# Taking GpSimd's library operations out of a decode attention kernel: masks from an identity on VectorE, maxima through VectorE transposes, totals through TensorE

## The chip, the cores and the metric

The kernel runs on one core of one Trainium2 chip. The metric is the device time of the slowest core, here the only one, in microseconds (us); lower is better. A core has five engines that run side by side: TensorE (PE in the profile; its weight loads are PEld), VectorE (DVE), ScalarE (ACT), GpSimd (POOL) and SyncE (SP). In this kernel SP issues the loads; 16 DMA engines carry them.

## The reference, cut to what matters

Four sequences each decode one token. The output is `g * a + (1 - g) * b`, where `a` is attention over a long cache and `b` a small gated MLP.

```python
def _A_ref(x, k_cache, v_cache, wq, wo):      # B=4, H=32 heads, Sk=8192 keys, Dh=128, bf16
    q = (x @ wq).reshape(B, Sq, H, Dh).transpose(0, 2, 1, 3)
    scores = jnp.einsum("bhqd,bhkd->bhqk", q, k_cache) * (Dh ** -0.5)
    p = _softmax(scores, axis=-1)
    o = jnp.einsum("bhqk,bhkd->bhqd", p, v_cache)
    return o.transpose(0, 2, 1, 3).reshape(B, Sq, H * Dh) @ wo
...
    g = _sigmoid((x * gate_w).sum(-1, keepdims=True))
    return g * a + (1 - g) * b
```

What matters is the size of the caches: K and V are 268 MB each, every byte is used once, and there is one query per head.

## The kernel before: the parts that the argument touches

Four heads of K (or of V) are one *pair* of loads. A pair fills two of the five slots of a ring in SBUF, 4.19 MB a slot. If the two slots are neighbours, the pair is a single load of 8.39 MB (line 194 of the kernel before); otherwise it is two loads of one slot each (line 198).

```python
NS = 5                                        # slots of the ring
def load_pair(src, n, apart=False):
    a = slots(2)
    if a + 1 < NS and not apart:
        lo = a * RING
        nc.sync.dma_start(out=flat[:, lo:lo + 2 * n], in_=src)              # L194: the whole pair
        return [flat[:, lo:lo + n], flat[:, lo + n:lo + 2 * n]]
    halves = [ring[:, a], ring[:, (a + 1) % NS]]
    for i, half in enumerate(halves):
        nc.sync.dma_start(out=half[:, 0:n], in_=src[:, i * n:(i + 1) * n])  # L198: one slot
    return halves
```

A K pair is worked off in eight chunks: VectorE transposes a chunk from the ring into one of three buffers, and PE multiplies it with `Z`, the spread-out queries. Four chunks empty one slot. After four K pairs (a *group*, eight groups in all) there is a softmax.

```python
def k_pair(d):                                # RD = 8 chunks, JT = 4 chunks a slot
    ...
    if d + 1 < ND:
        spread(d + 1)                         # L425, GpSimd: the Z of the next pair
    ks = load_pair(kv_view(A_k_cache, d), RING)
    for n in range(RD):
        kn, c = ks[n // JT], n % JT
        flat_t = turned(P, CJ * P)            # one of three buffers TB
        nc.vector.transpose(out=flat_t.bitcast(U32), in_=kn[...].bitcast(U32))       # L443
        for he in range(4):
            for z in range(2):
                nc.tensor.matmul(sps[:, z, :], lhsT=Z[...], rhs=T[...], ...)         # L449
        if n == JT + 2:
            flush_late()                      # runs the deferred reciprocal, among others
    if t == GD - 1:
        softmax(g)

def softmax(g):
    nc.vector.tensor_reduce(out=m1[:], in_=sps, axis=AX.X, op=ALU.max)               # L462
    nc.vector.scalar_tensor_tensor(out=mex[:], in0=mask, scalar=m1[:, 0:1], in1=pen[:], ...)
    nc.gpsimd.partition_all_reduce(gmx[:], mex[:], channels=P, reduce_op=bass_isa.ReduceOp.max)
    nc.vector.tensor_tensor(out=gmm[:], in0=gmx[:], in1=nmask[:], op=ALU.mult)
    nc.vector.tensor_reduce(out=negm[:], in_=gmm[:], axis=AX.X, op=ALU.add)
    nc.scalar.activation(out=PTs[:], in_=sps, func=ACT.Exp, bias=negm[:, 0:1], scale=scale,
                         accum_out=rs[:, 0:1])                                       # L474
    ...
    nc.gpsimd.partition_all_reduce(tot[:], rex[:], channels=P, reduce_op=bass_isa.ReduceOp.add)
    def inverse():
        nc.vector.reciprocal(out=rinv[:], in_=tot[:])                                # L484
    late.append(inverse)
```

A V pair needs only PE (64 matmuls, line 523). At the end of a group's V pairs ScalarE and VectorE scale the sums into `OS` (lines 535 and 536). The masks are made at the start with GpSimd's `affine_select`. TensorE, VectorE and GpSimd run in program order; ScalarE's order is chosen by the scheduler.

Of the kernel before, what the change touches and what calls it, by code (L numbers as in the profile page):

```python
# [9 lines left out]

BF = mybir.dt.bfloat16
F32 = mybir.dt.float32
U32 = mybir.dt.uint32
ACT = mybir.ActivationFunctionType
ALU = mybir.AluOpType
AX = mybir.AxisListType
# [98 lines left out]
def kernel(  # L115
# [15 lines left out]
    nc = tc.nc  # L131
    P = 128
# [4 lines left out]
    NQ = 4  # L137
    QP = P // NQ
    JR = Sk // QP // 2
    CJ = 32  # L140
    JT = JR // CJ
    RD = 2 * JT
    GD = QP // RD
    GH = GD * NQ
    ND = Bn * H // NQ
# [9 lines left out]
    scale = float(Dh) ** -0.5  # L155
# [3 lines left out]
    const = ctx.enter_context(tc.tile_pool(name="const", bufs=1))  # L159
    ptp = ctx.enter_context(tc.tile_pool(name="ptp", bufs=1))  # L160
    stat = ctx.enter_context(tc.tile_pool(name="stat", bufs=2))
# [15 lines left out]
    def turned(rows, n, dtype=BF):  # L177
        t = TB[tb_turn[0] % 3]
        tb_turn[0] += 1
        return t[0:rows, 0:n] if dtype == BF else t[0:rows, 0:2 * n].bitcast(dtype)  # L180
# [8 lines left out]
# [5 lines that stand above are left out]
            nc.sync.dma_start(out=flat[:, lo:lo + 2 * n], in_=src)  # L194
# [3 lines that stand above are left out]
            nc.sync.dma_start(out=half[:, 0:n], in_=src[:, i * n:(i + 1) * n])  # L198
        return halves

    def small(shape, dtype=F32):
        return mps.tile(shape, dtype, name="small", tag="small")
# [14 lines left out]
    for z in (q_ps, o_ps, acc4):  # L217
        nc.vector.memset(z[:], 0.0)
    acc = acc4[0:Bn].rearrange("p z n -> p (z n)")
    ident = const.tile([P, P], F32)  # L220
    make_identity(nc, ident[:])
    identb = const.tile([P, P], BF)
    nc.vector.tensor_copy(out=identb[:], in_=ident[:])
    xw_ps = small([P, DT, NX], BF)
# [3 lines left out]
    nc.vector.tensor_copy(out=xw[:], in_=xw_ps[:])  # L228
    xT = [xw[:, t, 0:Bn] for t in range(DT)]
    R = ptp.tile([P, 4, P], BF, name="R", tag="PTs")  # L230
    nc.gpsimd.memset(R[:], 0.0)
    for he in range(4):
        half, e = divmod(he, 2)
        nc.gpsimd.affine_select(out=R[:, he, :], in_=R[:, he, :], compare_op=ALU.not_equal, fill=1.0,
                                base=-(64 * half + e), pattern=[[0, 4], [-2, 32]], channel_multiplier=1)

    def band(t, width, steps):

        nc.gpsimd.memset(t[:], 1.0)
        nc.gpsimd.affine_select(out=t[:], in_=t[:], compare_op=ALU.is_ge, fill=0.0, base=0,  # L240
                                pattern=[[-s, n] for s, n in steps], channel_multiplier=1)
        nc.gpsimd.affine_select(out=t[:], in_=t[:], compare_op=ALU.is_ge, fill=0.0, base=width - 1,
                                pattern=[[s, n] for s, n in steps], channel_multiplier=-1)

    mask3 = const.tile([P, GD, NQ], F32)
    band(mask3, RD, [(RD, GD), (QP, NQ)])
    mask = mask3[:].rearrange("p t q -> p (t q)")
    pen = const.tile([P, GH], F32)
    nc.vector.tensor_scalar(out=pen[:], in0=mask, scalar1=-1.0, scalar2=3.0e38, op0=ALU.add, op1=ALU.mult)
    nmask = const.tile([P, GH], F32)  # L250
    nc.vector.tensor_scalar(out=nmask[:], in0=mask, scalar1=-scale, scalar2=None, op0=ALU.mult)
    selg = const.tile([P, 4, GD, NQ], F32)
    nc.gpsimd.memset(selg[:], 0.0)
    for e in range(2):
        nc.gpsimd.affine_select(out=selg[:], in_=selg[:], compare_op=ALU.not_equal, fill=1.0,
                                base=-16 * e, pattern=[[-1, 4], [-32, GD], [-4, NQ]], channel_multiplier=1)
    mE4 = const.tile([P, 2, 4], F32)
    band(mE4, 16, [(16, 2), (32, 4)])
    mE = const.tile([P, 2], F32)
    nc.vector.tensor_reduce(out=mE[:], in_=mE4[:], axis=AX.X, op=ALU.add)  # L260
    mq = const.tile([P, 1, NQ], BF)
    band(mq, QP, [(0, 1), (QP, NQ)])
    ZW = QP - 1 + P + 1
    Zt = [const.tile([P, 4, ZW], BF, name=f"Z{i}") for i in range(2)]
    PB = const.tile([P, QP, 2, 2, 2, NQ, 4], BF, name="PB")
# [149 lines left out]
    def heads(d):  # L415
        return divmod(d * NQ, H)

    def kv_view(cache, d):
        b, h0 = heads(d)
        return cache[b, h0:h0 + NQ].rearrange("h (r j) d -> (h r) (j d)", j=2 * JR)  # L420

    def spread(d):
        b, h0 = heads(d)
        Z = Zt[d % 2]
        nc.gpsimd.tensor_tensor(out=Z[:, :, QP - 1:QP - 1 + P].rearrange("p e (q c) -> p e q c", c=QP)[:, :, :, 0],  # L425
                                in0=qa[:, :, h0:h0 + NQ, b], in1=mq[:].to_broadcast([P, 4, NQ]), op=ALU.mult)

    def k_pair(d):
        g, t = divmod(d, GD)
        Z = Zt[d % 2]  # L430
        if d == 0:
            spread(0)
        if d + 1 < ND:
            spread(d + 1)
        if t == 0:
            S_ps[g] = scp.tile([P, 2, 512], F32, name="S_ps")
        sps = S_ps[g]
# [3 lines that stand above are left out]
            flat_t = turned(P, CJ * P)  # L441
            T = flat_t.rearrange("p (j h i e) -> p j h i e", j=CJ, h=2, e=2)
            nc.vector.transpose(out=flat_t.bitcast(U32),  # L443
                                in_=kn[:, c * CJ * Dh:(c + 1) * CJ * Dh].bitcast(U32))
            s = QP - 1 - (RD * t + n)
            for he in range(4):
                half, e = divmod(he, 2)
                for z in range(2):
                    nc.tensor.matmul(sps[:, z, :], lhsT=Z[:, he, s:s + P], rhs=T[:, 16 * z:16 * z + 16, half, :, e],  # L449
                                     start=(t == 0 and n == 0 and he == 0),  # L450
                                     stop=(t == GD - 1 and n == RD - 1 and he == 3))
            if n == JT:
                flush()
            if n == JT + 2:
                flush_late()
        if t == GD - 1:
            softmax(g)

    def softmax(g):
        sps = S_ps.pop(g)  # L460
        m1 = stat.tile([P, 1], F32, tag="m1")
        nc.vector.tensor_reduce(out=m1[:], in_=sps[:].rearrange("p z n -> p (z n)"), axis=AX.X, op=ALU.max)  # L462
        mex = stat.tile([P, GH], F32, tag="mex")
        nc.vector.scalar_tensor_tensor(out=mex[:], in0=mask, scalar=m1[:, 0:1], in1=pen[:],  # L464
                                       op0=ALU.mult, op1=ALU.add)
        gmx = stat.tile([P, GH], F32, tag="gmx")
        nc.gpsimd.partition_all_reduce(gmx[:], mex[:], channels=P, reduce_op=bass_isa.ReduceOp.max)  # L467
        gmm = stat.tile([P, GH], F32, tag="gmm")
        nc.vector.tensor_tensor(out=gmm[:], in0=gmx[:], in1=nmask[:], op=ALU.mult)
        negm = stat.tile([P, 1], F32, tag="negm")  # L470
        nc.vector.tensor_reduce(out=negm[:], in_=gmm[:], axis=AX.X, op=ALU.add)  # L471
        PTs = ptp.tile([P, 1024], BF, name="PTs", tag="PTs")
        rs = stat.tile([P, 1], F32, tag="rs")
        nc.scalar.activation(out=PTs[:], in_=sps[:].rearrange("p z n -> p (z n)"), func=ACT.Exp, bias=negm[:, 0:1], scale=scale, accum_out=rs[:, 0:1])  # L474
        PT = ptp.tile([P, 32, 32], BF, name="PT")
        nc.vector.transpose(out=PT[:].rearrange("p j i -> p (j i)"), in_=PTs[:])  # L476
        rex = stat.tile([P, GH], F32, tag="rex")
        nc.vector.tensor_scalar(out=rex[:], in0=mask, scalar1=rs[:, 0:1], scalar2=None, op0=ALU.mult)
        tot = stat.tile([P, GH], F32, tag="tot")
        nc.gpsimd.partition_all_reduce(tot[:], rex[:], channels=P, reduce_op=bass_isa.ReduceOp.add)  # L480

        def inverse():
            rinv = stat.tile([P, GH], F32, name="rinv", tag="rinv")
            nc.vector.reciprocal(out=rinv[:], in_=tot[:])  # L484
            rinv_t[g] = rinv
        late.append(inverse)

        def spread_p():
            Pv = PT[:].rearrange("p (q j) i -> p i q j", j=4)
            Bv = PB[:].rearrange("p i z w e s j -> p i (z w e) s j")  # L490
            for q in range(NQ):
                at = slice(QP * q, QP * (q + 1))
                if q % 2 == 0:
                    nc.scalar.copy(out=Bv[at, :, :, q, :], in_=Pv[at])  # L494
                else:
                    nc.gpsimd.tensor_copy(out=Bv[at, :, :, q, :], in_=Pv[at])  # L496
        behind.append(spread_p)
# [125 lines left out]
```

## Time and profile before

| what | before |
|---|---|
| time, median of the first 3 runs | 1344.0 us |
| bytes moved, mean rate | 576.18 MB, 429 GB/s |
| PE, DVE, ACT, POOL busy | 77%, 46%, 4%, 4% |

The page of the kernel before: busy time of each engine with its number of instructions, the busy tenths of the 16 DMA engines in 40 equal slices of the run, what they moved, and the shares of the chain of work that ended last.

```profile
span 1342.2 us, 7623 instructions
PE 1031.1 (77%) x4536; PEld 225.1 (17%) x2348; DVE 612.2 (46%) x358; ACT 50.6 (4%) x46; POOL 55.1 (4%) x90
DMA  9999999999999999999999999999999999999998
DMA packets 14316, 576.18 MB, mean 429 GB/s; under 512 B 1598, under 2 KB 1606, under 8 KB 2252
...
DMA 69%; DVE 19%; PE 10%; another core or an unknown queue 1%; issue 0%; ACT 0%; DVEq 0%; SPq 0%
```

The DMA row is the first thing to see: 9 tenths or more in 39 slices of 40. No other engine is near that. The chain still gives VectorE 19%. The next lines, from the chain of the kernel before in order of time (start, length, what), show why: four transposes free a slot, and a K load is issued at once.

```profile
327.45 8.90 DVE TB L443 x4
336.35 0.02 issue
336.37 29.65 DMA ring<-in_A_k_cache_dram
```

Four transposes free a slot at 336.35, a K load is issued at once, and it lands 29.65 us later. The timeline gives this issue as one instruction of line 194, so it is a whole pair of 8.39 MB. At 433 GB/s (the windows from 100 to 1200 us show 432 to 433), that is 19.4 us of transfer. The other 10 us passed mostly behind loads that were already queued: the load issued before it, at 315.02, landed 31.6 us later, at 346.6, and so had 10.3 us to go.

The softmax of one group, in the timeline of the kernel before (start, length, engine, line, operation; in brackets the idle time before it and its releaser):

```profile
618.43 1.22 DVE L462 TENSOR_REDUCE m<-S_ps 128x1 f32<-128x1024 f32 x1 [1.98 <-PE S_ps L449]
619.69 0.23 DVE L464 SCALAR_TENSOR_TENSOR mex<-mask,m,pen 128x16 f32<-128x16 f32 x1
620.06 0.39 POOL L467 PARTITION_ALL_REDUCE gmx<-mex  x1 [40.05 <-DVE mex L464]
620.49 0.18 DVE L469 TENSOR_TENSOR gmm<-gmx,nmask 128x16 f32<-128x16 f32 x1 [0.56 <-POOL gmx L467]
620.70 0.17 DVE L471 TENSOR_REDUCE negm<-gmm 128x1 f32<-128x16 f32 x1
620.90 1.11 ACT L474 ACTIVATE PTs<-S_ps,negm 128x1024 bf16<-128x1024 f32 x1 [136.73 <-DVE negm L471]
...
623.60 0.45 POOL L480 PARTITION_ALL_REDUCE tot<-rex  x1 [3.15 <-DVE rex L478]
624.08 0.25 DVE L484 RECIPROCAL rinv<-tot 128x16 f32<-128x16 f32 x1 [0.58 <-POOL tot L480]
```

The reductions themselves are short. What looks dear on GpSimd is something else: in the waits it sat idle with no releaser for 11.9 us before the first mask operation, and for 75.7 us in 7 cases before a spread that follows a reduction (engine, line, for what: total us, times, longest us):

```profile
POOL Z L425 <- issue: 75.7, 7, 12.3
```

The trace shows instructions named MODIFY_POOL_CONFIG at the reductions (16 records) and at the spreads (14). The Trainium skill ("GPSIMD Engine Reference", 2.1 Instruction dispatch) says that GpSimd's code can be loaded at run time, and that the first call of a freshly loaded one pays about 6 us with no visible instruction. The trace agrees in kind, and shows 10.8 us on average (75.7 / 7).

### The profile page before, as it was taken

How to read it: one execution, taken by the hardware profiler on the slowest of the kernel's cores; microseconds unless marked ns; L12 is line 12 of the kernel's file. 1: busy time of each engine (PE TensorE's matmuls, PEld its weight loads, DVE VectorE, ACT ScalarE, POOL GpSimd, SP SyncE). 2: the span in 40 equal slices, each digit the busy share in tenths (PEclk: the TensorE clock that was granted, in tenths of full speed). 3: DMA queues.
4: the chain of work that ended last, by engine and by line, in shares of the span. 5: the costliest groups of instructions: out<-in, count | busy, mean ns of one | idle time of the engine just before them, and what ended most of it. 6: DMA issues, size and time to landing. Idle time of an engine off the chain costs nothing.

```text
span 1342.2 us, 7623 instructions
## 1 busy us (share of the span) xinstructions
PE 1031.1 (77%) x4536; PEld 225.1 (17%) x2348; DVE 612.2 (46%) x358; ACT 50.6 (4%) x46; POOL 55.1 (4%) x90
## 2 busy tenths in 40 slices
PE   2565877787788687778977779697778679877898
PEld 0111111111111121111211112111111112111221
DVE  1555655544345554335455546146555254556000
ACT  0000100001000010001000010000100010000100
POOL 2000010001000010001000010000100010000100
PEclk9787988988998888899988889898889799889999
DMA  9999999999999999999999999999999999999998
GB/s 414 438 430 428 434 436 427 445 436 416 441 430 427 441 434 426 438 434 430 432 434 426 434 434 432 434 435 438 426 422 438 428 432 438 434 420 447 421 423 337
DMA packets 14316, 576.18 MB, mean 429 GB/s; under 512 B 1598, under 2 KB 1606, under 8 KB 2252
## 3 DMA queue, kind: packets, MB, share of 16 engines
q1 hardware_dynamic: 14276, 575.69, 99.5%
q8 instruction: 27, 0.44, 0.1%
q14 instruction: 5, 0.04, 0.0%
q10 hardware_dynamic: 8, 0.00, 0.0%
HBM read 575.68 MB, written 0.01 MB: 429 GB/s over the span
## 4 chain that ended last, share of the span: by engine, by line
DMA 69%; DVE 19%; PE 10%; another core or an unknown queue 1%; issue 0%; ACT 0%; DVEq 0%; SPq 0%
DMA ring<-in_A_k_cache_dram 56%; DVE TB L443 19%; DMA ring<-in_A_v_cache_dram 10%; PE o_ps L523 7%; PE S_ps L449 2%; DMA x<-in_A_x_dram 2%; DMA ring<-in_A_wo_dram 1%; PE S_ps L313 0%; PE acc L313 0%; PE acc L279 0%; PE small L543 0%; DVE OS L536 0%; ACT OS L535 0%; PE small L226 0%
## 5 line engine op out<-in xcount | busy, mean ns | idle before, releaser
L443 DVE STREAM_TRANSPOSE TB<-ring 128x2048 uint32<-128x2048 uint32 x256 | 567.0, 2277 | 494.6 <-DMA ring<-in_A_k_cache_dram 493.3
L449 PE MATMUL S_ps<-TB,Z 128*128 128x512 bf16 x2048 | 520.0, 410 | 218.5 <-DVE TB L443 218.2
L523 PE MATMUL o_ps<-ring,PB 128*32 128x512 bf16 x2048 | 460.0, 387 | 55.1 <-DMA ring<-in_A_v_cache_dram 50.5
L449 PEld LDWEIGHTS <-Z 128*128 128x128 bf16 x1024 | 105.6, 103 | 628.6 <-issue 627.0
L523 PEld LDWEIGHTS <-PB 128*32 128x32 bf16 x1024 | 100.6, 98 | 411.0 <-issue 402.1
L536 DVE SCALAR_TENSOR_TENSOR OS<-o_ps,mE,OS 128x512 f32<-128x512 f32 x8 | 6.0, 750 | 102.8 <-ACT OS L535 102.8
L474 ACT ACTIVATE PTs<-S_ps,negm 128x1024 bf16<-128x1024 f32 x8 | 8.9, 1113 | 1024.5 <-DVE negm L471 1024.5
L425 POOL TENSOR_TENSOR Z<-qa,mq 128x16 bf16<-128x16 bf16 x32 | 9.0, 285 | 745.1 <-PE S_ps L449 658.0
L496 POOL COPY PB<-PT 32x1024 bf16<-32x1024 bf16 x16 | 30.3, 1896 | 81.1 <-PE o_ps L523 80.7
L494 ACT COPY PB<-PT 32x1024 bf16<-32x1024 bf16 x16 | 30.6, 1909 | 1.5 <-DVE PT L476 1.3
L376 DVE CAST LT<-small 128x64 bf16<-128x64 f32 x2 | 0.4, 224 | 43.0 <-PE small L374 43.0
L226 PE MATMUL small<-identb,x 6*128 6x6 bf16 x8 | 0.7, 201 | 23.0 <-DMA x<-in_A_x_dram 23.0
L467 POOL PARTITION_ALL_REDUCE gmx<-mex x8 | 3.2, 394 | 340.3 <-DVE mex L464 340.3
L462 DVE TENSOR_REDUCE m<-S_ps 128x1 f32<-128x1024 f32 x8 | 9.8, 1224 | 15.9 <-PE S_ps L449 15.9
L279 PE MATMUL acc<-ring,LT 128*4 128x512 bf16 x64 | 14.8, 378 | 1.7 <-DMA ring<-in_A_wo_dram 0.9
L476 DVE STREAM_TRANSPOSE PT<-PTs 128x1024 bf16<-128x1024 bf16 x8 | 10.0, 1245 | 10.2 <-ACT PTs L474 10.2
L279 PE MATMUL acc<-ring,hT 128*4 128x512 bf16 x56 | 12.2, 379 | 0.0
L535 ACT ACTIVATE OS<-o_ps,mE 128x512 f32<-128x512 f32 x8 | 5.5, 687 | 159.0 <-PE o_ps L523 159.0
L313 PE MATMUL o_ps<-ring,xw 128*4 128x512 bf16 x56 | 6.3, 577 | 4.7 <-DMA ring<-in_B_w_gate_dram 4.7
L543 PEld LDWEIGHTS small<-selg,OS 128*128 128x128 f32 x64 | 8.2, 191 | 4.0 <-issue 3.9
L543 PE MATMUL small<-selg,OS 128*128 128x16 f32 x64 | 7.9, 255 | 0.0
L548 DVE SCALAR_TENSOR_TENSOR OT<-small,sgb,rinv 128x16 bf16<-128x16 f32 x8 | 1.8, 222 | 9.6 <-PE small L543 9.6
(71 smaller groups left out, 67.3 us busy)
## 6 DMA issues: line engine op xcount, KB each, us to landing
ring<-in_A_k_cache_dram SPq DMA_DIRECT2D x14, 4096.0 KB, 34.1
ring<-in_A_v_cache_dram SPq DMA_DIRECT2D x14, 4096.0 KB, 31.4
ring<-in_B_w_gate_dram SPq DMA_DIRECT2D x1, 7168.0 KB, 38.0
ring<-in_B_w_up_dram SPq DMA_DIRECT2D x1, 7168.0 KB, 39.2
ring<-in_B_w_down_dram SPq DMA_DIRECT2D x2, 3584.0 KB, 28.0
ring<-in_A_wo_dram SPq DMA_DIRECT2D x6, 1024.0 KB, 24.7
ring<-in_A_v_cache_dram SPq DMA_DIRECT2D x2, 2048.0 KB, 30.9
ring<-in_A_v_cache_dram SPq DMA_DIRECT2D x4, 1024.0 KB, 24.6
```

The source lines that it names most:

```text
L279: nc.tensor.matmul(out_ap, lhsT=lhsT, rhs=rhs, start=start, stop=True, skip_group_check=True)
L313: nc.tensor.matmul(ps[32 * k:32 * k + Bn, z, :], lhsT=xT[TW * half + t], rhs=cols(w, t, 4 * z + k), start=(half + t == 0), stop=(half == 1 ...
L425: nc.gpsimd.tensor_tensor(out=Z[:, :, QP - 1:QP - 1 + P].rearrange("p e (q c) -> p e q c", c=QP)[:, :, :, 0], in0=qa[:, :, h0:h0 + NQ, b], ...
L443: nc.vector.transpose(out=flat_t.bitcast(U32), in_=kn[:, c * CJ * Dh:(c + 1) * CJ * Dh].bitcast(U32))
L449: nc.tensor.matmul(sps[:, z, :], lhsT=Z[:, he, s:s + P], rhs=T[:, 16 * z:16 * z + 16, half, :, e], start=(t == 0 and n == 0 and he == 0), ...
L462: nc.vector.tensor_reduce(out=m1[:], in_=sps[:].rearrange("p z n -> p (z n)"), axis=AX.X, op=ALU.max)
L474: nc.scalar.activation(out=PTs[:], in_=sps[:].rearrange("p z n -> p (z n)"), func=ACT.Exp, bias=negm[:, 0:1], scale=scale, accum_out=rs[:, ...
L476: nc.vector.transpose(out=PT[:].rearrange("p j i -> p (j i)"), in_=PTs[:])
L494: nc.scalar.copy(out=Bv[at, :, :, q, :], in_=Pv[at])
L496: nc.gpsimd.tensor_copy(out=Bv[at, :, :, q, :], in_=Pv[at])
L523: nc.tensor.matmul(o_ps[row:row + NM, e, :], lhsT=PB[:, RD * t + c, z, w].rearrange("p e s j -> p (e s j)"), rhs=vn[:, j0 * Dh:(j0 + 4) * ...
L543: nc.tensor.matmul(oT[:, :], lhsT=o_sb[:, q * Dh:(q + 1) * Dh], rhs=selg[:, q].rearrange("p t s -> p (t s)"), start=(q == 0), stop=(q == 3))
```

## The change

The intent is to leave GpSimd nothing but memsets and copies. An identity is made on VectorE from an index row and its transpose; every mask is a sum or a copy of parts of it. A head has 8 of the 128 rows of scores; its maximum is taken by transposing 32x32 blocks (four heads each) on VectorE, reducing over 8 columns at a time, and transposing back. The totals are a matmul with a matrix of ones. The Z spreads move to VectorE.

```diff
-    make_identity(nc, ident[:])
+    nc.vector.tensor_scalar(out=row[:, n:2 * n], in0=row[:, 0:n], scalar1=float(n), ..., op0=ALU.add)   # doubling
+    nc.vector.transpose(out=col[:].bitcast(U32), in_=row[:, 0:32].bitcast(U32))
+    nc.vector.tensor_scalar(out=ident[:], in0=row[:], scalar1=col[:, 0:1], scalar2=None, op0=ALU.is_equal)
 ... (R, mask, selg, mE, mq: affine_select on GpSimd -> copies, adds and reductions of ident on VectorE)
-        nc.gpsimd.tensor_tensor(out=Z[...], in0=qa[...], in1=mq[...], op=ALU.mult)
+        nc.vector.tensor_tensor(out=Z[...], in0=qa[...], in1=mq[...], op=ALU.mult)
 ... (in k_pair: the spread moves from the head of the pair to after its third transpose)
-        nc.gpsimd.partition_all_reduce(gmx[:], mex[:], channels=P, reduce_op=bass_isa.ReduceOp.max)
+        nc.vector.transpose(out=mxT[:].bitcast(U32), in_=mx[:].bitcast(U32))
+        nc.vector.tensor_reduce(out=gm[:], in_=mxT[:].rearrange("p (t r) -> p t r", r=RD), axis=AX.X, op=ALU.max)
+        nc.vector.tensor_scalar(out=ng[...], in0=gm[:].unsqueeze(2).to_broadcast([P, GD, RD]), scalar1=-scale, ...)
+        nc.vector.transpose(out=ngT[:].bitcast(U32), in_=ng[:].bitcast(U32))
-        nc.gpsimd.partition_all_reduce(tot[:], rex[:], channels=P, reduce_op=bass_isa.ReduceOp.add)
         def inverse():
+            tot = small([P, GH])
+            nc.tensor.matmul(tot[:, :], lhsT=ones[:], rhs=rex[:], start=True, stop=True)
             nc.vector.reciprocal(out=rinv[:], in_=tot[:, :])
```

`inverse` is called later than it is written, so the matmul stands in PE's program at that later place, and VectorE, which runs in program order too, stops at the reciprocal until PE gets there.

More of the change, by code (lines that the diff above doesn't have):

```diff
@@ L6 @@
 from concourse import bass_utils, mybir
-from concourse.bass import bass_isa
-from concourse.masks import make_identity
 from concourse._compat import with_exitstack
@@ L219 @@
     acc = acc4[0:Bn].rearrange("p z n -> p (z n)")
+    row = const.tile([P, P], F32)
+    nc.vector.memset(row[:, 0:1], 0.0)
+    n = 1
+    while n < P:
+        nc.vector.tensor_scalar(out=row[:, n:2 * n], in0=row[:, 0:n], scalar1=float(n), scalar2=None, op0=ALU.add)
+        n *= 2
+    col = const.tile([P, 32], F32)
+    nc.vector.transpose(out=col[:].bitcast(U32), in_=row[:, 0:32].bitcast(U32))
+    for n in range(32, P, 32):
+        nc.vector.tensor_scalar(out=col[n:n + 32], in0=col[n:n + 32], scalar1=float(n), scalar2=None, op0=ALU.add)
     ident = const.tile([P, P], F32)
-    make_identity(nc, ident[:])
+    nc.vector.tensor_scalar(out=ident[:], in0=row[:], scalar1=col[:, 0:1], scalar2=None, op0=ALU.is_equal)
     identb = const.tile([P, P], BF)
@@ L230 @@
     R = ptp.tile([P, 4, P], BF, name="R", tag="PTs")
-    nc.gpsimd.memset(R[:], 0.0)
-    for he in range(4):
-        half, e = divmod(he, 2)
-        nc.gpsimd.affine_select(out=R[:, he, :], in_=R[:, he, :], compare_op=ALU.not_equal, fill=1.0,
-                                base=-(64 * half + e), pattern=[[0, 4], [-2, 32]], channel_multiplier=1)
-    def band(t, width, steps):
-        nc.gpsimd.memset(t[:], 1.0)
-        nc.gpsimd.affine_select(out=t[:], in_=t[:], compare_op=ALU.is_ge, fill=0.0, base=0,
-                                pattern=[[-s, n] for s, n in steps], channel_multiplier=1)
-        nc.gpsimd.affine_select(out=t[:], in_=t[:], compare_op=ALU.is_ge, fill=0.0, base=width - 1,
-                                pattern=[[s, n] for s, n in steps], channel_multiplier=-1)
+    for half in range(2):
+        for e in range(2):
+            turns = ident[:, 64 * half + e:64 * half + 64:2]
+            for n in range(4):
+                nc.vector.tensor_copy(out=R[:, 2 * half + e, 32 * n:32 * n + 32], in_=turns)
@@ L245 @@
     mask3 = const.tile([P, GD, NQ], F32)
-    band(mask3, RD, [(RD, GD), (QP, NQ)])
+    nc.vector.tensor_reduce(out=mask3[:], in_=ident[:].rearrange("p (q t r) -> p t q r", q=NQ, t=GD), axis=AX.X, op=ALU.add)
     mask = mask3[:].rearrange("p t q -> p (t q)")
-    pen = const.tile([P, GH], F32)
-    nc.vector.tensor_scalar(out=pen[:], in0=mask, scalar1=-1.0, scalar2=3.0e38, op0=ALU.add, op1=ALU.mult)
-    nmask = const.tile([P, GH], F32)
-    nc.vector.tensor_scalar(out=nmask[:], in0=mask, scalar1=-scale, scalar2=None, op0=ALU.mult)
@@ L252 @@
     selg = const.tile([P, 4, GD, NQ], F32)
-    nc.gpsimd.memset(selg[:], 0.0)
-    for e in range(2):
-        nc.gpsimd.affine_select(out=selg[:], in_=selg[:], compare_op=ALU.not_equal, fill=1.0,
-                                base=-16 * e, pattern=[[-1, 4], [-32, GD], [-4, NQ]], channel_multiplier=1)
+    one = ident[:].rearrange("p (t e s a) -> p e a t s", t=GD, e=2, s=NQ)
+    for a in range(4):
+        nc.vector.tensor_tensor(out=selg[:, a], in0=one[:, 0, a], in1=one[:, 1, a], op=ALU.add)
@@ L257 @@
     mE4 = const.tile([P, 2, 4], F32)
-    band(mE4, 16, [(16, 2), (32, 4)])
+    nc.vector.tensor_reduce(out=mE4[:], in_=ident[:].rearrange("p (n e r) -> p e n r", n=4, e=2), axis=AX.X, op=ALU.add)
     mE = const.tile([P, 2], F32)
     nc.vector.tensor_reduce(out=mE[:], in_=mE4[:], axis=AX.X, op=ALU.add)
+    mq4 = const.tile([P, NQ], F32)
+    nc.vector.tensor_reduce(out=mq4[:], in_=ident[:].rearrange("p (q r) -> p q r", q=NQ), axis=AX.X, op=ALU.add)
     mq = const.tile([P, 1, NQ], BF)
-    band(mq, QP, [(0, 1), (QP, NQ)])
+    nc.vector.tensor_copy(out=mq[:, 0, :], in_=mq4[:])
@@ L263 @@
+    ones = const.tile([P, P], F32)
+    nc.gpsimd.memset(ones[:], 1.0)
+    mx, mxT, ng, ngT = [const.tile([P, 32], F32, name=f"mx{i}") for i in range(4)]
+    nc.vector.memset(mx[:], 0.0)
     ZW = QP - 1 + P + 1
@@ L424, in spread @@
         Z = Zt[d % 2]
-        nc.gpsimd.tensor_tensor(out=Z[:, :, QP - 1:QP - 1 + P].rearrange("p e (q c) -> p e q c", c=QP)[:, :, :, 0],
+        nc.vector.tensor_tensor(out=Z[:, :, QP - 1:QP - 1 + P].rearrange("p e (q c) -> p e q c", c=QP)[:, :, :, 0],
                                 in0=qa[:, :, h0:h0 + NQ, b], in1=mq[:].to_broadcast([P, 4, NQ]), op=ALU.mult)
@@ L432, in k_pair @@
             spread(0)
-        if d + 1 < ND:
-            spread(d + 1)
         if t == 0:
@@ L451, in k_pair @@
                                      stop=(t == GD - 1 and n == RD - 1 and he == 3))
+            if n == JT // 2 and d + 1 < ND:
+                spread(d + 1)
             if n == JT:
@@ L460, in softmax @@
         sps = S_ps.pop(g)
-        m1 = stat.tile([P, 1], F32, tag="m1")
-        nc.vector.tensor_reduce(out=m1[:], in_=sps[:].rearrange("p z n -> p (z n)"), axis=AX.X, op=ALU.max)
-        mex = stat.tile([P, GH], F32, tag="mex")
-        nc.vector.scalar_tensor_tensor(out=mex[:], in0=mask, scalar=m1[:, 0:1], in1=pen[:],
-                                       op0=ALU.mult, op1=ALU.add)
-        gmx = stat.tile([P, GH], F32, tag="gmx")
-        nc.gpsimd.partition_all_reduce(gmx[:], mex[:], channels=P, reduce_op=bass_isa.ReduceOp.max)
-        gmm = stat.tile([P, GH], F32, tag="gmm")
-        nc.vector.tensor_tensor(out=gmm[:], in0=gmx[:], in1=nmask[:], op=ALU.mult)
-        negm = stat.tile([P, 1], F32, tag="negm")
-        nc.vector.tensor_reduce(out=negm[:], in_=gmm[:], axis=AX.X, op=ALU.add)
+        nc.vector.tensor_reduce(out=mx[:, 0:1], in_=sps[:].rearrange("p z n -> p (z n)"), axis=AX.X, op=ALU.max)
+        nc.vector.transpose(out=mxT[:].bitcast(U32), in_=mx[:].bitcast(U32))
+        gm = stat.tile([P, GD], F32, tag="gm")
+        nc.vector.tensor_reduce(out=gm[:], in_=mxT[:].rearrange("p (t r) -> p t r", r=RD), axis=AX.X, op=ALU.max)
+        nc.vector.tensor_scalar(out=ng[:].rearrange("p (t r) -> p t r", r=RD), in0=gm[:].unsqueeze(2).to_broadcast([P, GD, RD]),
+                                scalar1=-scale, scalar2=None, op0=ALU.mult)
+        nc.vector.transpose(out=ngT[:].bitcast(U32), in_=ng[:].bitcast(U32))
+        negm = ngT
         PTs = ptp.tile([P, 1024], BF, name="PTs", tag="PTs")
@@ L478, in softmax @@
         nc.vector.tensor_scalar(out=rex[:], in0=mask, scalar1=rs[:, 0:1], scalar2=None, op0=ALU.mult)
-        tot = stat.tile([P, GH], F32, tag="tot")
-        nc.gpsimd.partition_all_reduce(tot[:], rex[:], channels=P, reduce_op=bass_isa.ReduceOp.add)
         def inverse():
+            tot = small([P, GH])
+            nc.tensor.matmul(tot[:, :], lhsT=ones[:], rhs=rex[:], start=True, stop=True)
             rinv = stat.tile([P, GH], F32, name="rinv", tag="rinv")
-            nc.vector.reciprocal(out=rinv[:], in_=tot[:])
+            nc.vector.reciprocal(out=rinv[:], in_=tot[:, :])
             rinv_t[g] = rinv
```

## The prediction

> **What bounds the kernel now.** Memory traffic. The page shows the 16 DMA engines at 9 tenths or more in 39 of 40 slices, 576.18 MB at a mean of 429 GB/s; the windows from 100 to 1200 us show 432 to 433 GB/s and a DMA share of 1.00. 576.18 MB at 433 GB/s is 1331 us, which leaves 11 us of the 1342.2 us span for start, tail and small dips. The Trainium skill ("DMA: Bandwidth & Descriptors", Where 436 GB/s comes from) gives 435 GB/s as the ceiling of a core's DMA fabric; the trace agrees. PE is 77% busy, DVE 46%, GpSimd 4%. The chain of waits names DVE transposes for 19%, but only because a transpose frees the slot that the next load fills: a 4.19 MB half lands 29.7 us after its issue and needs 9.7 us at 433 GB/s, so some 20 us of loads are queued ahead of it (for a whole pair 34.1 - 19.4 = 15 us). A later issue costs nothing until that queue is used up.
>
> **What changes.**
> - Start: the identity waited for GpSimd until 13.2 us (11.9 us idle before its first select). On VectorE it is ready by about 6 us (estimate: memsets end at 4.1, then a dozen ops of 0.1 to 0.3 us). No gain: the first transposes wait for x, which lands at 22.98. The other masks (about 4 us by estimate) stand behind the xw copy, from 23.9 to about 28 us; the next VectorE work is due at 29.7. Even a miss of 2 us is absorbed: the first K pair lands at 50.0.
> - Maxima, 8 times: before, 1.25 us from the end of the reduction to Exp. After: two transposes, a reduction, a scaling, about 0.2 us each. Gain at most 0.4 us x 8, off the critical path.
> - Totals: 8 GpSimd reductions (0.45 us) become fp32 matmuls of about 0.3 us; PE is 23% idle. The reciprocal now waits for PE's place in the program: once (first group) 2 to 4 us amid a K pair; for the others it stands before an operation that waits for the end of the V pair anyway.
> - Z spreads, 32 times: from GpSimd (0.26 us) to VectorE (about 0.2 us), after the third transpose, whose own wait for PE covers theirs. VectorE total about 612 + 6 + 5 = 623 us.
> - GpSimd: all reductions go, and the idle time with no releaser before its spreads (75.7 us in 7 cases, up to 12.3 us, which looks like switching its program). Only 5.2 us of PE's waits name GpSimd. Left: memsets and 16 copies, about 36 us busy.
>
> **Critical path.** None of it, apart from noise. The same bytes move by the same queue entries in the same order, and the tail after the last load (about 5 us) is unchanged.
>
> **Prediction.** 1343.5 us, 8 in 10 within 1340 to 1347. Faster by over 2%: 0.01; within 2%: 0.98; slower by over 2%: 0.01.
>
> **What the profile would show.** Mean rate 428 to 431 GB/s, all slices but the last at 9. Identity ready before 8 us, first PE work still at 23 us. GpSimd about 36 us busy, VectorE 618 to 632 us. The first group's reciprocal waiting 2 to 4 us for PE; first K transpose still at about 50 us. No wait for a releaser on the spreads.
>
> **What would make it wrong.** A VectorE wait for PE over 10 to 15 us, which drains the load queue; the R masks running well past 30 us and pushing the Q chain beyond the first K pair; or a change of DMA rate from placement or less fetch traffic, which I expect under 0.3%.

## More of the kernel before

The chain follows one wait back to its releaser; it does not say how much later the releaser could have come. The list of its loads (`--dma`) has the K loads by size, with the median time in us from issue to landing; the 14 loads of 4096 KB are single slots (line 198), the other 25 are pairs (line 194):

```profile
ring<-in_A_k_cache_dram SPq DMA_DIRECT2D x14, 4096.0 KB, 34.1
ring<-in_A_k_cache_dram SPq DMA_DIRECT2D x25, 36.7
```

In the chain the pairs take from 28.4 to 40.4 us, so the load shown is one of the quicker ones, with less ahead of it than the others.

## The result, and the profile after

The changed kernel took 1344.08 us (median of 6 runs), the kernel before 1343.91 us (median of 6 runs). The ratio is 1.0002, with a 95% interval of 0.9989 to 1.0015. (A ratio here is the mean time of one kernel's fast runs over that of the other's of the same rounds, so it is not quite the ratio of the medians.) The time did not change.

The same lines of the page, of the kernel after:

```profile
span 1342.0 us, 7617 instructions
PE 1037.2 (77%) x4552; PEld 228.1 (17%) x2364; DVE 621.8 (46%) x434; ACT 50.6 (4%) x46; POOL 35.5 (3%) x24
DMA  9999999999999999999999999999999999999997
DMA packets 14316, 576.18 MB, mean 429 GB/s; under 512 B 1598, under 2 KB 1606, under 8 KB 2252
...
DMA 69%; DVE 19%; PE 11%; issue 0%; ACT 0%; SPq 0%; DVEq 0%
```

GpSimd lost 19.6 us of work and 66 of its 90 instructions; VectorE gained 9.6 us and PE 6.1 us. The bytes, the rate and the packets are the same to the last digit.

The same softmax, in the timeline of the kernel after:

```profile
618.32 1.22 DVE L464 TENSOR_REDUCE mx<-S_ps 128x1 f32<-128x1024 f32 x1 [1.98 <-PE S_ps L449]
619.58 0.21 DVE L465 STREAM_TRANSPOSE mx<-mx 128x32 uint32<-128x32 uint32 x1
619.82 0.19 DVE L467 TENSOR_REDUCE gm<-mx 128x4 f32<-128x32 f32 x1
620.04 0.18 DVE L468 TENSOR_SCALAR mx<-gm 128x32 f32<-128x32 f32 x1
620.26 0.21 DVE L470 STREAM_TRANSPOSE mx<-mx 128x32 uint32<-128x32 uint32 x1
620.51 1.11 ACT L474 ACTIVATE PTs<-S_ps,mx 128x1024 bf16<-128x1024 f32 x1 [135.69 <-DVE mx L470]
...
625.22 0.40 PE L482 MATMUL small<-rex,ones 128*128 128x16 f32 x2
625.55 7.08 PE L523 MATMUL o_ps<-ring,PB 128*32 128x512 bf16 x32
625.65 0.26 DVE L484 RECIPROCAL rinv<-small 128x16 f32<-128x16 f32 x1 [2.55 <-PE small L482]
```

From the end of the row maximum (619.54) to Exp it is now 0.97 us, before 1.25 us (620.90 - 619.65). The reciprocal, which had waited 0.58 us for GpSimd, waits 2.55 us for PE here. Over the run that wait is large. From the waits (engine, line, for whom: total us, times, longest us), first two of the kernel before, then two of the kernel after:

```profile
DVE OS L536 <- ACT OS L535: 102.8, 8, 20.1
DVE rinv L484 <- POOL tot L480: 4.1, 7, 0.6
DVE OS L536 <- ACT OS L535: 70.8, 8, 18.5
DVE rinv L484 <- PE small L482: 41.5, 8, 13.8
```

Before, the reciprocal waited 4.1 us for GpSimd and `OS` 102.8 us for ScalarE. So of the 37.4 us by which the reciprocal's wait grew, 32.0 us were taken from the wait of the operation that follows it on VectorE. It moved a wait rather than made one. But one of these waits was 13.8 us, and the prediction had named 10 to 15 us as what would drain the queue. That wait, before the reciprocal at 473.36 us, is followed by 7.47 us more for `OS`, so VectorE could not have gone on earlier without it. The experiments ask how much delay the queue does bear.

### The profile page after: what moved, and what is told of

Same layout as the page of the kernel before. It is cut to its first block, busy times and chain, and to the rows that moved or that the text cites. A ratio compares the mean times of both kernels' runs of the same rounds, so it can differ in the third digit from the quotient of the medians.

```text
span 1342.0 us, 7617 instructions
## 1 busy us (share of the span) xinstructions
PE 1037.2 (77%) x4552; PEld 228.1 (17%) x2364; DVE 621.8 (46%) x434; ACT 50.6 (4%) x46; POOL 35.5 (3%) x24
## 3 DMA queue, kind: packets, MB, share of 16 engines
HBM read 575.68 MB, written 0.01 MB: 429 GB/s over the span
## 4 chain that ended last, share of the span: by engine, by line
DMA 69%; DVE 19%; PE 11%; issue 0%; ACT 0%; SPq 0%; DVEq 0%
DMA ring<-in_A_k_cache_dram 58%; DVE TB L443 19%; DMA ring<-in_A_v_cache_dram 7%; PE o_ps L523 7%; PE S_ps L449 3%; DMA ring<-in_B_w_gate_dram 3%; DMA ring<-in_A_wo_dram 1%; PE o_ps L315 0%; DVE Z L427 0%; PE acc L315 0%; PE acc L281 0%; PE small L482 0%; PE small L543 0%; DVE OS L536 0%; ACT OS L535 0%
## 5 line engine op out<-in xcount | busy, mean ns | idle before, releaser
L474 ACT ACTIVATE PTs<-S_ps,mx 128x1024 bf16<-128x1024 f32 x8 | 8.9, 1114 | 1019.7 <-DVE mx L470 1019.7
L235 PE MATMUL small<-identb,x 6*128 6x6 bf16 x8 | 0.6, 197 | 22.2 <-DMA x<-in_A_x_dram 22.2
L464 DVE TENSOR_REDUCE mx<-S_ps 128x1 f32<-128x1024 f32 x8 | 9.8, 1225 | 15.9 <-PE S_ps L449 15.9
L315 PE MATMUL S_ps<-ring,xw 128*4 128x512 bf16 x64 | 6.3, 582 | 0.3 <-DVE xw L237 0.3
```

The source lines that it names most:

```text
L315: nc.tensor.matmul(ps[32 * k:32 * k + Bn, z, :], lhsT=xT[TW * half + t], rhs=cols(w, t, 4 * z + k), start=(half + t == 0), stop=(half == 1 ...
L464: nc.vector.tensor_reduce(out=mx[:, 0:1], in_=sps[:].rearrange("p z n -> p (z n)"), axis=AX.X, op=ALU.max)
L474: nc.scalar.activation(out=PTs[:], in_=sps[:].rearrange("p z n -> p (z n)"), func=ACT.Exp, bias=negm[:, 0:1], scale=scale, accum_out=rs[:, ...
```

## The experiments

Theory A: the loads bound the time, and all of the change lies behind the queue of loads. Rival B: gains and losses of the change are real and cancel. Rival C: VectorE's share of the chain is a real bound. The remaining theories are named where they arise. Each batch of four runs shares its runs of the kernel before (1343.79 to 1343.86 us).

### One part undone: the spreads back to GpSimd

```diff
-        nc.vector.tensor_tensor(out=Z[...],
+        nc.gpsimd.tensor_tensor(out=Z[...],
```

> The changed kernel with one part undone: the 32 Z spreads go back to GpSimd, at their new place in the program. Theory A (the loads bound the time, everything changed lies behind the queue of loads): 1344, within 2 us of both kernels. Rival B (gains and losses of the change cancel; the spread on VectorE is one of the losses, 6.0 us of VectorE work): faster than the changed kernel by 3 to 6 us.

Measured: 1344.05 us, ratio to the kernel before 1.0002 (0.9987 to 1.0016). VectorE's work fell to 619.4 us and GpSimd's rose to 44.4 us; the time did not move. Rival B needs a loss here that could be given back; there is none in the spreads. The other parts are taken up below, with fewer bytes.

### Fewer bytes

`part` makes a pair load only a share of each slot; the rest of the slot holds old data. The result is wrong.

```diff
-    ks = load_pair(kv_view(A_k_cache, d), RING)
+    ks = load_pair(kv_view(A_k_cache, d), RING, part=(7, 8) if d >= 4 else None)
 ... (V the same, without the last pair)
```

> Wrong result on purpose: the changed kernel with 59 of 64 K and V pairs loading 7/8 of each slot, 61.9 MB fewer, 514.3 MB in all; nothing else differs. Theory A (bytes bound the time): 514.3 MB at 433 GB/s is 1188 us, and 11 us of start, tail and dips as before: 1199, at most 1215 because PE is then 87% busy. A theory in which the loop is held by the chain of transposes and matmuls and not by bytes: 1300 or more.

Measured: 1206.08 us, ratio 0.8975, 7 us above the forecast. The page of this run:

```profile
DMA  9999999999999999999999999999999999999997
DMA packets 20204, 514.31 MB, mean 427 GB/s; under 512 B 1598, under 2 KB 1606, under 8 KB 2252
```

10.7% of the bytes went, and 10.3% of the time with them; the rate (427 against 429 GB/s) and the full DMA row stayed, although the shorter loads are cut into more packets. All the compute instructions were still there (7617). This is the bound.

### How deep is the queue? Extra transposes

The first four (or two, or three) transposes of each K pair are done twice. The second writes the same values.

```diff
             nc.vector.transpose(out=flat_t.bitcast(U32), in_=kn[...].bitcast(U32))
+            if n < JT:                       # n < 2 and n < 3 in the other runs
+                nc.vector.transpose(out=flat_t.bitcast(U32), in_=kn[...].bitcast(U32))
```

> The changed kernel with each of the first four K transposes of a pair done twice: 128 more operations of about 2.2 us, so about 282 us more VectorE work (622 to about 904 us busy, 67%) and every release of a slot 9 us later. Theory A: the queue of loads is 15 to 20 us deep, so 1344 to 1349. Rival C (the chain's 19% of VectorE is a real bound, VectorE work counts in full in that part of the loop): 1400 or more.

Measured: 1430.9 us, ratio 1.0647. That is 87 us more, and my reading of the margin fell. I had taken the load that lands 29.7 us after its issue for a slot of 4.19 MB, which made 20 us of queue. It is a pair. The windows of the run with four extra transposes, just before and after such a pair is issued at 617.12 us (stretch, length, busy us of the engines, PE clock, DMA share, GB/s):

```profile
610.00:615.00 5.00, 4.03 (x10) 0.72 (x5) 4.93 (x5) 0.00 (x0) 0.00 (x0) 0.50 0.97 419
615.00:617.00 2.00, 1.10 (x3) 0.14 (x1) 2.00 (x1) 0.00 (x0) 0.00 (x0) 0.68 0.09 33
617.00:620.00 3.00, 2.55 (x12) 0.49 (x6) 3.00 (x3) 0.00 (x0) 0.00 (x0) 1.00 1.02 350
```

From 615 to 617 us hardly a packet began (a share of 0.09) while VectorE was busy all the time: the queue had run dry. A window counts a packet where it begins, and the packets here last 2.42 us, so by the trace's packets the engines ran on until about 616; the new load's first large packet began at 618.07, and they stood still for some 2 us. The chain of the same run gives what a pair's load takes when nothing is ahead of it:

```profile
617.12 21.80 DMA ring<-in_A_k_cache_dram
702.25 23.08 DMA ring<-in_A_k_cache_dram
```

The line 617.12 gives 21.8 us (21.9 us was used in the expectations), so the queue that such a pair can lose in the plain kernel is about 29.7 - 21.9 = 7.8 us, not 20. (The 10.3 us that were still to be loaded at its issue agree: a load that meets an empty queue takes some 2.4 us more than its 19.4 us of transfer, so it must be issued that much before the queue ends.) Call this theory E. Two smaller doses test it.

> The changed kernel with the first two K transposes of a pair done twice: 64 more operations, about 144 us more VectorE work, each release 4.5 us later. Theory E (the queue ahead of a pair's load is 29.7 - 21.9 = 7.8 us deep, 21.9 us being what such a load took in the run with four extra, when it met an empty queue): 4.5 is less than 7.8, so 1344 to 1350. Rival C (VectorE work counts): half of the 87 us that four extra cost, 1380 to 1390.

Measured: 1349.34 us, ratio 1.0037. It fits E; rival C's 1380 does not.

> The changed kernel with the first three K transposes of a pair done twice: 96 more operations, about 216 us more VectorE work, each release 6.8 us later, 1 us short of the 7.8 us of the queue. Theory E: 1345 to 1375, the knee of the curve. Rival C: three quarters of 87 us, 1405 to 1412.

Measured: 1384.14 us, ratio 1.0303. The knee (the delay at which time begins to be lost) is near where E puts it, but the run is 9 us above E's range, so the usable margin is less than 7.8 us: between 4.6 and 6.8 us by the table.

| extra transposes a pair | release later by (estimate, 2.28 us each) | VectorE busy | time |
|---|---|---|---|
| 0 | 0 | 621.8 us | 1344.08 us |
| 2 | 4.6 us | 768.5 us | 1349.34 us |
| 3 | 6.8 us | 842.6 us | 1384.14 us |
| 4 | 9.1 us | 917.0 us | 1430.9 us |

The first 147 us of VectorE work cost 5 us; the next 74 us cost 35 us and the next 74 us cost 47 us. VectorE was idle for over a third of the span in every one of these runs.

### Did the change use up the margin?

The kernel before with the same three extra transposes, with ScalarE held to program order (its order in the full kernel).

> The kernel before (ScalarE in program order, its own) with the first three K transposes of a pair done twice, as the run of the changed kernel that took 1384.1. If the change does not use up the queue's margin: 1378 to 1386, the difference no more than the 0.1 to 0.2 us by which a spread now delays a release, at some 20 us of run per us of delay. Rival G (the change leaves the kernel with much less margin, which the plain runs do not show): below 1370.

Measured: 1379.64 us, ratio 1.0263. The changed kernel with the same load is 4.5 us slower (1384.14; another batch, whose runs of the kernel before differ by 0.07 us). Rival G falls: the margin is nearly the same in both. The 4.5 us suggest that a small part is used up, which plain runs cannot show; at 20 us of run per us of delay they are 0.2 us. Which part of the change takes it was not tested.

### What the change is worth where the loads do not bound the time

With half of each slot loaded, 247 MB fewer, the DMA engines are no longer full, and PE is the busiest engine (89% of the span in the run of 1096.44 us below).

> Wrong result on purpose: the kernel before, but 59 of the 64 K and V pairs load only the first half of each slot (the other half keeps old data), 247 MB fewer of 576 MB. Theory A: the loads then need about 760 us at 433 GB/s and no longer bound the time; PE, with 1031 us busy, does: 1060 to 1200 us. It is the base for the next run.

Measured: 1116.92 us, ratio 0.8311.

> Wrong result on purpose: the changed kernel with the same 247 MB left out. Theory A: what the change is worth off the memory bound shows here; I expect it within 15 us of the run before it: PE has 8 small matmuls more and VectorE waits for PE before each reciprocal (41.5 us in the full kernel), GpSimd's switching (75.7 us idle) is gone. Rival B (gains and losses cancel at full size by chance): the difference is about nought here too only if each part is small; a difference over 15 us shows that the parts are real and that the loads hid them.

Measured: 1101.36 us, ratio 0.8196. Taken alone this says that the change gains 15.6 us once the loads are out of the way. It does not. The timeline of the first of these two runs, the kernel before:

```profile
519.82 0.17 DVE L476 TENSOR_REDUCE negm<-gmm 128x1 f32<-128x16 f32 x1
...
531.46 0.69 ACT L540 ACTIVATE OS<-o_ps,mE 128x512 f32<-128x512 f32 x1 [117.92 <-PE o_ps L528]
532.05 1.11 ACT L479 ACTIVATE PTs<-S_ps,negm 128x1024 bf16<-128x1024 f32 x1
```

Exp had its maximum at 520 us and ran at 532, because ScalarE's instructions stood in another order: the scaling of `OS`, which waits for the end of a V pair, came first. In the full kernels Exp comes first, and so it does in the trace of every other run here, those with extra transposes included. The scheduler had chosen anew when I changed the loads, in the kernel before and not in the changed one. So the pair was run again with ScalarE in program order:

```diff
-    engines={mybir.EngineType.PE, mybir.EngineType.DVE, mybir.EngineType.Pool}
+    engines={mybir.EngineType.PE, mybir.EngineType.DVE, mybir.EngineType.Pool, mybir.EngineType.Activation}
```

> Wrong result on purpose: as the first half-load run of the kernel before, but ScalarE's instructions keep the order of the program (Exp of a softmax before the OS scaling of the next V pair), as they have in the full-size kernels; in that first run the scheduler had put OS ahead of Exp, and Exp waited up to 13.3 us. If that order made the run slow, this one is 10 to 16 us faster than 1116.9: 1101 to 1107.

Measured: 1096.44 us, ratio 0.8154, 20.5 us faster and so below the range: the order cost more than I had expected.

> Wrong result on purpose: the changed kernel, half loads, ScalarE in program order, which is the order it had in its own first half-load run: 1101.4 again, within 2 us. Theory A': off the memory bound the change itself is worth less than 6 us, and the 15.6 us between the first two half-load runs was ScalarE's order. Rival D: the change itself is worth 10 us or more there, then the run before stays 10 us or more above this one.

Measured: 1101.23 us, ratio 0.8193. Rival D falls, and even the sign is turned: without the memory bound the change costs 4.8 us. (The changed kernel has the same order in both of its half-load runs; on two chips they differ by 0.13 us.)

### Where those 4.8 us come from

Theory F: the place of the totals on PE. In the changed half-load run, where the first group's reciprocal stands in the middle of a K pair:

```profile
177.41 1.90 PE L454 MATMUL S_ps<-TB,Z 128*128 128x512 bf16 x8 [0.30 <-DVE TB L448]
179.14 0.29 PE L487 MATMUL small<-rex,ones 128*128 128x16 f32 x2
179.47 0.26 DVE L489 RECIPROCAL rinv<-small 128x16 f32<-128x16 f32 x1 [2.12 <-PE small L487]
179.64 8.82 DVE L448 STREAM_TRANSPOSE TB<-ring 128x2048 uint32<-128x2048 uint32 x4
181.95 1.89 PE L454 MATMUL S_ps<-TB,Z 128*128 128x512 bf16 x8 [2.52 <-DVE TB L448]
```

VectorE had been ahead of PE. It stops 2.12 us for PE, and then PE stops 2.52 us for the transpose that could not be made in that time. One part was undone: the totals go back to GpSimd's reduction, all else stays.

```diff
-            tot = small([P, GH])
-            nc.tensor.matmul(tot[:, :], lhsT=ones[:], rhs=rex[:], start=True, stop=True)
+        tot = stat.tile([P, GH], F32, tag="tot")
+        nc.gpsimd.partition_all_reduce(tot[:], rex[:], channels=P, reduce_op=bass_isa.ReduceOp.add)
```

> Wrong result on purpose: half loads, ScalarE in program order, the changed kernel with one part undone: the totals go back to the GpSimd reduction. Theory F (the 4.8 us by which the changed kernel is slower there come from the totals' place on PE: one stop of some 2.5 us in the first group and 8 breaks of PE of about 0.5 us): 1095 to 1098. If another part of the change is the cause: 1100 to 1102.

Measured: 1095.97 us, ratio 0.8155, the time of the kernel before under the same conditions. So the totals are the 4.8 us, and the masks, the maxima and the spreads together are nought there within the spread of such runs (about 3 us). How the 4.8 us divide between the one stop and the eight breaks of PE was not separated; PE's whole wait for transposes is 74.3 us in the kernel before, 76.7 us in the changed one and 75.2 us with the totals back on GpSimd.

The second test was to move the matmul and the reciprocal to a better place.

```diff
-        late.append(inverse)
+        inv_t[g] = inverse                   # the last group keeps late.append
 ... (in finish, after the gathering matmuls)
+            late.append(inv_t.pop(g))
```

> Wrong result on purpose: half loads, ScalarE in program order, the changed kernel with the matmul of the total and the reciprocal moved to where the group's output is gathered (after a pair of matmul groups that PE breaks for anyway); only the last group keeps its place. Theory F says that the wait of the reciprocal (20.0 us in all) goes, and with it the stop in the first group: 1097 to 1100. If the wait costs nothing: 1101.

Measured: 1120.67 us, ratio 0.8339: 19.4 us slower instead of faster. The edit did not do what I wrote. What is put into `late` there is run two chunks on, in the middle of the next K pair, so instead of one group most groups got the stop that only the first had had. PE's wait for transposes, first in the changed half-load run (ScalarE in program order), then in this one:

```profile
PE S_ps L454 <- DVE TB L448: 76.7, 73, 12.6
PE S_ps L455 <- DVE TB L449: 90.9, 77, 12.7
```

It rose by 14.2 us; in the timeline one such stop of PE is 2.83 us, so that is five more of them, and the timeline has six reciprocals in the middle of a K pair instead of one. The expectation was wrong. Read after the fact, the miss supports F: a PE result that VectorE needs in the middle of a K pair costs about 3 us each time once PE is the limit. The other 5 of the 19.4 us are matched in size by the K matmuls themselves, which were busy for 487.9 us instead of 481.9, at a mean granted clock of 0.956 instead of 0.963; why the clock was lower no run shows.

## Why the prediction was right, and where its steps were off

The time, 1343.5 us with a range of 1340 to 1347, was right: 1344.08 us.

- *"What bounds the kernel now. Memory traffic."* Right. The run with fewer bytes shows it: 10.7% fewer bytes, 10.3% less time, at the same full DMA row. The Trainium skill ("DMA: Bandwidth & Descriptors", Where 436 GB/s comes from) names 435 GB/s as the ceiling of a core's DMA fabric; the long windows show 432 to 434. The same section says that for transfers between HBM and SBUF the HBM side, about 358 GB/s, is what binds. The prediction passed over this, and the trace contradicts it: the page shows 575.68 MB read from HBM at 429 GB/s over the span. The measurement decides.
- *"some 20 us of loads are queued ahead of it"* Wrong. I had the two sizes crosswise. The load of 29.7 us that I read as a slot is a pair, and what it can lose is at most 7.8 us; the median of 34.1 us that I took for pairs, and so "15 us", is that of single slots. The knee of the doses lies between 4.6 and 6.8 us of delay. The conclusion held only because the change delays a release by much less: 0.19 us for a spread, and 2.12 us once, for the first reciprocal. That it did not come near the true margin was no merit of this step. "A VectorE wait for PE over 10 to 15 us, which drains the load queue" was likewise set too high for a wait that stands in front of transposes that are due.
- *Start.* Right. The identity was ready at 7.7 us, VectorE's last mask operation ended at 25.8 us (I had said 28), and the first K transpose began at 49.87 us (before: 49.99). The first PE work came at 22.2 instead of 23.0 us, which changed nothing.
- *Maxima.* Right: 0.97 us instead of 1.25 us in the group shown.
- *Totals.* Right in mechanism. The first group's reciprocal waited 2.12 us amid a K pair. The other waits were longer than I had in mind (up to 13.8 us), but stood, as said, before an operation that waits for the end of the V pair anyway; 32.0 us of them came out of that operation's own wait.
- *Spreads, VectorE and GpSimd sums.* Right: 0.189 us a spread with no idle time before them, 621.8 us on VectorE (623), 35.5 us on GpSimd (36).
- *GpSimd's idle time of 75.7 us is free.* Right. It is gone, and the time is the same. The half-load runs agree: there it was 53.4 us in the kernel before, and there too the change gains nothing by its going.

Not tested: the masks and the maxima each by itself. Nor does the comparison with the reference prove the new maxima and totals right, since it passed the runs with missing loads too; that they compute the same is read from the code. Not run: a version that beats both kernels. No experiment pointed to one, because all that the change touches is hidden behind the loads.

## What to carry to other kernels

When one resource is full from the first slice to the last, as the loads are here, ask of a change first whether it delays that resource; cleaning up an engine beside it, here 75 us of idle time, was worth nothing. The margin behind which work hides can be measured: add a known dose of work and find the knee, and check which size of load you are reading before you compute a queue from its time to landing. And if you take a bound away to see what lies beneath, compare the instruction orders first: here a scheduler's choice made 15.6 us of gain out of a change that costs 4.8 us.

## What the Trainium skill lacked or had wrong

- "GPSIMD Engine Reference", 2.1 Instruction dispatch, gives about 6 us for the first call of freshly loaded code. In the kernel before, GpSimd was idle with no releaser for 11.9 us before its first mask operation and for 75.7 us in 7 cases between a reduction and a spread, 10.8 us each (longest 12.3). It does not say what brings the cost back: here it came each time the kernel went from reductions to spreads, and not at all in the loop when only one of the two kinds was left on GpSimd (2 MODIFY_POOL_CONFIG records instead of 32).
- "GPSIMD Engine Reference", 4. When to use GPSIMD, calls GpSimd the only option for reductions across partitions, and "VectorE: DVE Perf Modes", Why `tensor_reduce` can't reduce along partition axis, sends the reader to GpSimd. Two other ways were used here: a maximum over blocks of partitions by two VectorE transposes of 128x32 (0.21 us each), a reduction (0.19 us) and a scaling (0.18 us), and a sum by two passes of PE over a matrix of ones (0.29 to 0.40 us for both).
- "Perfetto Trace Analysis", What "DMA-bound" means, does not tell how to measure how late a load may be issued before a DMA-bound kernel slows down. Here that margin was between 4.6 and 6.8 us of a period of 39 us (from one K pair's load to the next), and past it each us of delay of a release cost about 15 to 21 us of run (35 us and then 47 us for 2.28 us each, by estimate).
